# Feed-forward block 0: from the fourth weight group on, the low parts of the weights are made by GpSimd instead of VectorE

## The chip, the core and the metric

The kernel runs on one core of a Trainium2 chip. The metric is the device time of one execution in microseconds (us). TensorE (PE), VectorE (DVE), ScalarE (ACT), GpSimd (POOL) and SyncE (SP) each work through an instruction queue of their own, in order, and wait for each other through semaphores. GpSimd has two jobs here: it computes, and it issues one of the two large families of DMAs (SyncE issues the other).

## The reference, cut to what matters

A residual block of 2048 tokens and 576 channels, with a modulation by `c` and two sublayers. The first is a long convolution (S4D: a kernel `K` is generated from `log_A_real`, `A_imag`, `C` and `log_dt`, and applied by FFT); the second is a dense feed-forward layer with a hidden width of 4608 and ReLU:

```python
h = _layernorm(x) * (1 + ca) + sa
x = x + ga * _A_ref(h, ...)            # long convolution, output gated
h = _layernorm(x) * (1 + cb) + sb
x = x + gb * (maximum(h @ w1, 0) @ w2)  # 576 -> 4608 -> 576
```

Everything is float32. The kernel reaches that precision on TensorE with a rounded format, float32r: an operand is split into a high part (the value rounded to float32r) and a low part (the value minus the high part), and a product is made of three: high by high, high by low, low by high.

## The kernel before, in words

The tokens are cut into NB = 4 blocks of 512. The feed-forward layer goes block by block, and the hidden width goes in NF = 36 groups of 128, so that there are 144 groups in all, numbered `g`. A group has 14 matmuls of 128x512 into the hidden tile `hps` (`first`, line 1217 in the profile of before), a ReLU on ScalarE that gives the high part `hh` (L1222), one VectorE instruction that gives the low part `hl` (L1223), and 14 matmuls of 128x512 into five accumulators `acc0` to `acc4` (`second`, L1242), two groups later.

**Weights.** A group has a tile of `w1` (128x640) and one of `w2` (128x576). SyncE loads the raw values into `r1` (L1176) and `r2` (L1180), ScalarE copies them to the high part (`split1`, L1192, and `split2`, L1201), and VectorE subtracts the high from the raw part to get the low part (in the profile all of these have line 490, that of the helper `v`, and read `w<-r,w`). `split1(g + 2)` and `split2(g)` are called in turn `g` of the main loop, and the tiles are used in turn `g + 2`, so that each is asked for two groups ahead of its use. The low parts are made only in block 0 (`g < NF`): they are also stored to `L1d` and `L2d` (L1293, from SyncE), and blocks 1 to 3 load them from there. `r1`, `r2`, `w1` and `w2` have three buffers each, so that the load of a raw tile waits until the low part of the third group before it has been made.

**Beside the feed-forward of a block** runs the convolution of the next one. For block 0 this is `block0()`: first `kg.rest`, which makes the rest of the convolution kernel (VectorE multiplies in `rot`, L389 to L395, then small TensorE products `kps<-W1r,W2r`, L421), then the storing of the kernel `kd` to memory and its loading as `kt`, and `conv(1)`: transforms on TensorE (`ps_f`, L725), butterflies and products on VectorE (tiles `W`, `U`, `K`, `Y`, `T`, `V`, all with line 490), and the inverse transform on TensorE (`ps_i`, L955). After the second inverse come the layer norm and the transposes (`ps_t`, L1006) that make block 1's operands `xh`, `xl`, `xs`. Block 1's first matmul waits for `xs`.

**GpSimd's queue** holds in this part of the program only DMA issues: loads for `kg.rest` (`W`, `Zr`, `W2r`, L379 to L381), stores of spectra (`Ud`, `Rd`, `Kd`, L716), and loads of spectra (`Ua`, `Ka`, `R`, L712). An issue that waits for its data or its buffer holds up what stands behind it. In conv(1) `Us`, `Ks` and `Vs` of the two halves p = 0 and 1 of the channels are handled one after the other; the product of half p (`product`, `Y` and `T`) needs `Ua<-Ud_0_p` and `Ka`, which come back from memory.

**Order.** The program is written as generators, which `step` advances by small pieces; then a scheduler places all instructions of an engine in one order, by their dependencies and by its own estimate of what each instruction takes. Thus moving one instruction to another engine also changes the order in which others stand, on every engine.

Of the kernel before, what the change touches and what calls it, by code (L numbers as in the profile page):

```python
# [14 lines left out]
ALU = mybir.AluOpType  # L15
# [5 lines left out]
D = 576  # L21
# [446 lines left out]
class Body:  # L468
# [20 lines left out]
    def v(self, *args, **kw):  # L489
        return self.kept(self.nc.vector.tensor_tensor(*args, **kw))  # L490
# [675 lines left out]
    def ffn(self, gens):  # L1166

        nc, I, ff = self.nc, self.I, self.ff
        v = self.v
# [8 lines left out]
        def load_r2(g):  # L1178
            r2[g] = ff.tile([P, D], F32, tag="r2", bufs=3, name="r2")
            self.kept(nc.sync.dma_start(out=r2[g], in_=I["w2"][(g % NF) * P : (g % NF) * P + P, :]))  # L1180

        def low1(g):
            w = w1[g] = ff.tile([P, 2, 5, P], F32R, tag="w1", bufs=3, name="w1")
            if g >= NF:
                nc.sync.dma_start(
                    out=w[:, 1].rearrange("p k c -> p (k c)").bitcast(F32), in_=self.L1d[g % NF]
                )

        def split1(g):

            w, r = w1[g], r1.pop(g)
            nc.scalar.activation(w[:, 0], r, AF.Copy)  # L1192
            if g < NF:
                v(w[:, 1], r, w[:, 0], op=ALU.subtract)
                late.append((self.L1d[g], w[:, 1].rearrange("p k c -> p (k c)")))

        def split2(g):

            w = w2[g] = ff.tile([P, 1152], F32R, tag="w2", bufs=3, name="w2")
            r = r2.pop(g)  # L1200
            nc.scalar.activation(w[:, 0:D], r, AF.Copy)  # L1201
            if g < NF:
                v(w[:, D:640], r[:, 512:D], w[:, 512:D], op=ALU.subtract)
                v(w[:, 640:], r[:, :512], w[:, :512], op=ALU.subtract)
                late.append((self.L2d[g], w[:, D:]))
            else:
                nc.sync.dma_start(out=w[:, D:].bitcast(F32), in_=self.L2d[g % NF])
# [71 lines left out]
        for g in range(3):  # L1279
            low1(g)  # L1280
        split1(0)
        split2(0)
        split1(1)
        yield
        waiting = []
        for g in range(n + 2):
            if g < n:
                if g + 3 < n:
                    load_r1(g + 3)
                if g + 2 < n:  # L1290
                    load_r2(g + 2)
                for dst, src in late:
                    nc.sync.dma_start(out=dst, in_=src.bitcast(F32))  # L1293
                late.clear()
                if g:
                    split2(g)
                if g and g + 2 < n:
                    split1(g + 2)
                waiting.append((g, *first(g)))
                if g == 0:  # L1300
                    split1(2)
                if g + 3 < n:
                    low1(g + 3)
                step(g)
# [164 lines left out]
```

## Time and profile before

| | |
|---|---|
| median of 3 runs | 1395.86 us (1393.40 to 1396.19) |
| the profiled execution | 1396.13 us |
| its span, first to last instruction | 1394.4 us |
| mean granted TensorE clock | 0.937 |
| PE busy | 1233.8 us, 88% |
| DVE busy | 877.9 us, 63% |
| ACT busy | 500.6 us, 36% |
| POOL busy | 197.0 us, 14% |

The feed-forward of block 0 goes from 237 us (the first `hps` matmul) to 585 us (the first `hps` matmul of block 1) of the span. Before that lie the set-up and the convolution of block 0, behind it blocks 1 to 3.

How to read the rows shown further on. A row of groups reads: line, engine, operation, output<-inputs by the program's names (buffer numbers left out), shapes, xcount | busy us in all, mean ns of one | idle time of the engine just before them, and what ended it. A row of the timeline reads: start in us, length in us, engine, line, operation, tiles, xcount, and in brackets the idle time before it and who ended it; consecutive instructions of one kind are merged. A row of stretches reads: from:to in us, length, then busy us and (xcount) of PE, PEld (weight load), DVE, ACT and POOL, then the granted TensorE clock, the share of the DMA engines and GB/s. A row of waits reads: engine, tile and line that waited <- whom it waited for: us in all, times, the longest. Consecutive VectorE instructions overlap by some 0.08 us in the records, so that several in a row take a little less than their count by their mean.

### The profile page before, as it was taken

What the parts mean: (1) busy time and instruction counts of PE and PEld (TensorE: products, weight loads), DVE (VectorE), ACT (ScalarE), POOL (GpSimd) and SP (SyncE); (2) the same over time, 40 slices, a digit from 0 to 9 for tenths busy, and PEclk for the clock granted to TensorE, in tenths of its full rate; (3) what the DMA queues carried; (4) which work ended last, traced back from release to release, by engine and by line L of the source; (5) the groups of instructions that cost most, each with busy time, mean ns of one, the idle gap of its engine ahead of it and who ended that gap; (6) DMA issues with size and microseconds to landing.
All of it is one profiled execution on the core that took longest, in us unless ns stands there. A gap on an engine that the chain in (4) does not pass through costs nothing. (4 is left out here: it accounts for less than half of the span.)

```text
span 1394.4 us, 26020 instructions
## 1 busy us (share of the span) xinstructions
PE 1233.8 (88%) x10600; PEld 978.6 (70%) x10600; DVE 877.9 (63%) x1352; ACT 500.6 (36%) x1006; POOL 197.0 (14%) x268
## 2 busy tenths in 40 slices
PE   5124677999999988889999989999999999999998
PEld 3123455777787767567777877777887878888886
DVE  5978968999885698659834978264899332101011
ACT  6975224222223322422234314543322353323231
POOL 1877311011111101021011010000010000000000
PEclk9555688999999999899999999999999999999999
DMA  6665778688878859499778996676988656666651
GB/s 191 237 240 210 274 278 308 230 297 310 286 277 276 307 196 343 148 314 343 253 244 305 339 347 198 188 251 194 377 310 308 194 161 204 204 199 195 199 176 60
DMA packets 136040, 347.55 MB, mean 249 GB/s; under 512 B 23472, under 2 KB 23760, under 8 KB 135920
## 3 DMA queue, kind: packets, MB, share of 16 engines
q1 hardware_dynamic: 108688, 222.75, 49.3%
q0 software_dynamic: 26944, 122.55, 23.9%
q8 instruction: 83, 1.36, 0.4%
q10 hardware_dynamic: 288, 0.59, 0.1%
q14 instruction: 37, 0.30, 0.1%
HBM read 264.44 MB, written 81.40 MB: 248 GB/s over the span
## 5 line engine op out<-in xcount | busy, mean ns | idle before, releaser
L1242 PE MATMUL acc<-hh,w 128*128 128x512 f32 x1296 | 424.3, 402 | 5.7 <-DVE w L490 5.7
L1217 PE MATMUL hps<-xh,w 128*128 128x512 f32 x1152 | 393.1, 401 | 0.4 <-ACT xh L1018 0.4
L1242 PEld LDWEIGHTS acc<-hh,w 128*128 128x128 f32 x1296 | 243.4, 189 | 59.6 <-DVE w L490 7.4
L1242 PE MATMUL acc<-hl,w 128*128 128x512 f32 x720 | 279.4, 400 | 0.0
L1223 DVE SCALAR_TENSOR_TENSOR hl<-hps,hh 128x512 fp32r<-128x512 f32 x144 | 98.7, 685 | 284.2 <-ACT hh L1222 284.0
L1217 PEld LDWEIGHTS hps<-xh,w 128*128 128x128 f32 x1152 | 216.5, 189 | 47.4 <-ACT xh L1018 1.2
L1217 PE MATMUL hps<-xl,w 128*128 128x512 f32 x576 | 229.8, 399 | 0.2 <-DVE xl L1023 0.2
L1222 ACT ACTIVATE hh<-hps 128x512 fp32r<-128x512 f32 x144 | 86.0, 598 | 339.7 <-PE hps L1217 336.8
L1201 ACT ACTIVATE w<-r 128x576 fp32r<-128x576 f32 x144 | 98.7, 686 | 225.7 <-issue 176.7
L1242 PEld LDWEIGHTS acc<-hl,w 128*128 128x128 f32 x720 | 135.7, 189 | 28.5
L1217 PEld LDWEIGHTS hps<-xl,w 128*128 128x128 f32 x576 | 108.8, 189 | 24.2 <-DVE xl L1023 0.5
L246 PE MATMUL kps<-W,W 128*32 128x16 f32 x2304 | 40.0, 218 | 90.8 <-POOL W L59 58.8
L1192 ACT ACTIVATE w<-r 128x640 fp32r<-128x640 f32 x144 | 105.4, 732 | 26.2 <-DMA r<-in_w_dram 25.0
L246 PEld LDWEIGHTS kps<-W,W 128*32 128x32 f32 x2304 | 37.7, 151 | 94.1 <-POOL W L59 60.1
L1217 PE MATMUL hps<-xs,w 128*128 128x512 f32 x288 | 97.3, 418 | 6.2 <-DVE hl L1223 5.5
L421 PEld LDWEIGHTS kps<-W1r,W2r 128*32 128x32 f32 x3456 | 68.9, 146 | 35.0 <-issue 21.3
L421 PE MATMUL kps<-W1r,W2r 128*32 128x48 f32 (+2 forms) x3456 | 78.0, 238 | 11.2 <-issue 5.9
L490 DVE TENSOR_TENSOR Y<-Y,T 128x1152 f32<-128x1152 f32 x64 | 84.9, 1349 | 0.2
L1217 PEld LDWEIGHTS hps<-xs,w 128*128 128x128 f32 x288 | 53.6, 192 | 20.2 <-DVE hl L1223 7.5
L726 ACT ACTIVATE Z<-ps_f 128x288 f32<-128x288 f32 x104 | 42.1, 408 | 69.0 <-PE ps_f L725 63.0
L490 DVE TENSOR_TENSOR w<-r,w 128x512 fp32r<-128x512 f32 (+2 forms) x108 | 57.8, 570 | 8.7 <-ACT w L1201 8.7
L955 PE MATMUL ps_i<-V,gc 128*128 128x288 f32 x136 | 45.4, 469 | 15.2 <-DVE x L490 12.6
(203 smaller groups left out, 1368.5 us busy)
## 6 DMA issues: line engine op xcount, KB each, us to landing
r<-in_w_dram SPq DMA_DIRECT2D x144, 320.0 KB, 4.0
r<-in_w_dram SPq DMA_DIRECT2D x144, 288.0 KB, 3.6
w<-L1d SPq DMA_DIRECT2D x108, 320.0 KB, 3.0
w<-L2d SPq DMA_DIRECT2D x108, 288.0 KB, 3.4
W2r<-W2d POOLq DMA_DIRECT2D x18, 1536.0 KB, 9.0
W2d<-W SPq DMA_DIRECT2D x12, 1536.0 KB, 7.7
Ua<-Ud POOLq DMA_DIRECT2D x15, 1152.0 KB, 11.1
W<-W1d POOLq DMA_DIRECT2D x18, 768.0 KB, 9.0
```

The lines of the kernel that those rows point to most:

```text
L246: self.nc.tensor.matmul(ps[32 * dd : 32 * dd + 32, 12 * u + q, :], W2[:, r, :, ch], W1[:, u, :, r, ch], start=(r == 0), stop=(r == 1),)
L421: nc.tensor.matmul(ps[32 * dd : 32 * dd + 32, q, :], W2[:, r, :, ch], W1[:, :na, r, ch], start=(r == 0), stop=(r == 1),)
L490: return self.kept(self.nc.vector.tensor_tensor(*args, **kw))
L726: nc.scalar.activation(Z[:, n2, c], ps[:, :PC], AF.Copy)
L955: self.nc.tensor.matmul(ps[:, :PC], a, b, start=(i == 0), stop=(i == len(todo) - 1))
L1192: nc.scalar.activation(w[:, 0], r, AF.Copy)
L1201: nc.scalar.activation(w[:, 0:D], r, AF.Copy)
L1217: nc.tensor.matmul(ps, a, x, start=(i == 0), stop=(i == 13))
L1222: nc.scalar.activation(hh, ps, AF.Relu)
L1223: nc.vector.scalar_tensor_tensor(hl, ps, 0.0, hh, op0=ALU.max, op1=ALU.subtract)
L1242: nc.tensor.matmul(acc[i], a, x, start=(f == 0 and j in (0, 3, 6, 9, 12)), stop=(f == NF - 1 and j in (2, 5, 8, 11, 13)),)
```

## The change

Both splits no longer call VectorE's subtract themselves but a new helper `low`, which takes VectorE for the groups 0 to 2 and GpSimd for the groups 3 to 35. Operands, results, tiles, buffers and the stores behind them stay as they are. Each group has three such subtracts: 128x640 for `w1`, and 128x64 and 128x512 for `w2`. So 33 x 3 = 99 instructions change the engine.

```diff
@@ -1179,6 +1179,10 @@ def ffn
+        def low(g, out, r, hi):
+            f = v if g < 3 else nc.gpsimd.tensor_tensor
+            f(out, r, hi, op=ALU.subtract)
+
@@ -1191,7 +1195,7 @@ def split1
             nc.scalar.activation(w[:, 0], r, AF.Copy)
             if g < NF:
-                v(w[:, 1], r, w[:, 0], op=ALU.subtract)
+                low(g, w[:, 1], r, w[:, 0])
                 late.append((self.L1d[g], w[:, 1].rearrange("p k c -> p (k c)")))
@@ -1200,8 +1204,8 @@ def split2
             nc.scalar.activation(w[:, 0:D], r, AF.Copy)
             if g < NF:
-                v(w[:, D:640], r[:, 512:D], w[:, 512:D], op=ALU.subtract)
-                v(w[:, 640:], r[:, :512], w[:, :512], op=ALU.subtract)
+                low(g, w[:, D:640], r[:, 512:D], w[:, 512:D])
+                low(g, w[:, 640:], r[:, :512], w[:, :512])
                 late.append((self.L2d[g], w[:, D:]))
```

In the changed kernel all lines behind the new helper stand four lines lower: L1217 becomes L1221, L1242 becomes L1246, and so on; the subtracts on GpSimd have line L1184.

## The prediction, before the changed kernel was run

> **What bounds the kernel now.** First I read the waits of TensorE, since it is busy for 88% of the span; then the stretches of block 0; then, in the stretch where it waits, what VectorE and GpSimd do. In the view of stretches the columns are from:to, length, busy us of PE, PEld, DVE, ACT and POOL with counts, granted clock, DMA share, GB/s:
>
> ```profile
> 250.00:400.00 150.00, 144.80 (x2324) 114.65 (x2323) 136.62 (x143) 34.20 (x64) 19.73 (x30) 0.99 0.78 271
> 400.00:490.00 90.00, 88.45 (x715) 67.18 (x714) 61.59 (x110) 31.77 (x67) 13.98 (x20) 1.00 0.87 301
> 490.00:564.00 74.00, 61.03 (x259) 47.87 (x258) 67.65 (x86) 16.63 (x28) 4.50 (x6) 0.98 0.68 246
> 564.00:585.00 21.00, 20.20 (x76) 14.87 (x76) 13.04 (x39) 10.41 (x21) 0.00 (x0) 0.84 0.63 201
> 1200.00:1225.00 25.00, 25.00 (x112) 20.71 (x111) 2.58 (x4) 7.56 (x12) 0.00 (x0) 1.00 0.68 199
> ```
>
> Up to 490 us and again from 564 us TensorE is busy nearly all the time. Only from 490 to 564 is it idle for 13.0 us, and there VectorE is busy for 67.65 of 74 us. The last row, from block 3, gives the price of a matmul of 128x512 where nothing disturbs: 25 us / 112 = 0.223 us.
>
> Whom TensorE waits for between 490 and 585 us (total, times, longest):
>
> ```profile
> PE acc L1242 <- DVE w L490: 5.7, 3, 5.0
> PE hps L1217 <- DVE hl L1223: 5.1, 3, 2.0
> PE ps_i L955 <- DVE V L490: 2.6, 1, 2.6
> ```
>
> The first row is the one that the change takes away. But the longest of these waits is directly followed by the one for `V`, which is the input of the second inverse transform: TensorE gets there by 561 us and `V` is there at 564 us. From `V` the way goes through `ps_i`, norm and transposes to block 1. So what sets block 0's end is when VectorE has made `V`, plus the TensorE work that stands behind `ps_i` in its queue. The waits for `w` and `hl` before it are time that TensorE would have spent waiting for `V` instead.
>
> What lies on VectorE's way to `V`, from the groups of VectorE between 490 and 564 us:
>
> ```profile
> L490 DVE TENSOR_TENSOR T<-Ka,Ua 128x1152 f32<-128x1152 f32 x4 | 5.2, 1352 | 2.9 <-issue 2.9
> L490 DVE TENSOR_TENSOR T<-K,Ua 128x1152 f32<-128x1152 f32 x4 | 5.2, 1352 | 3.0 <-DMA Ua<-Ud 3.0
> L490 DVE TENSOR_TENSOR Y<-K,Ua 128x1152 f32<-128x1152 f32 x4 | 5.2, 1350 | 5.3 <-issue 5.3
> L490 DVE TENSOR_TENSOR w<-r,w 128x640 fp32r<-128x640 f32 x6 | 4.9, 815 | 0.0
> L1223 DVE SCALAR_TENSOR_TENSOR hl<-hps,hh 128x512 fp32r<-128x512 f32 x7 | 4.8, 681 | 0.0
> L490 DVE TENSOR_TENSOR w<-r,w 128x512 fp32r<-128x512 f32 x6 | 4.1, 682 | 0.0
> L490 DVE TENSOR_TENSOR x<-ps_i,x 128x288 f32<-128x288 f32 x4 | 1.8, 451 | 0.1
> L490 DVE TENSOR_TENSOR w<-r,w 128x64 fp32r<-128x64 f32 x7 | 1.5, 215 | 0.0
> ```
>
> The low parts are 4.9 + 4.1 + 1.5 = 10.5 us of it, and 5.3 + 3.0 + 2.9 = 11.2 us are idle, each time ahead of a product that reads `Ua`, a load that GpSimd issues. GpSimd's timeline around them:
>
> ```profile
> 475.15 0.77 POOL L716 DMA_DIRECT2D Rd<-K  x1 [4.05 <-DVE K L490]
> 478.41 0.76 POOL L716 DMA_DIRECT2D Kd<-K  x1 [2.48 <-DVE K L861]
> 479.16 0.76 POOL L712 DMA_DIRECT2D Ua<-Ud  x1
> 509.27 0.75 POOL L712 DMA_DIRECT2D R<-Rd  x1 [28.61 <-DVE T L490]
> 524.18 0.76 POOL L716 DMA_DIRECT2D Rd<-K  x1 [14.16 <-DVE K L490]
> 524.93 0.75 POOL L712 DMA_DIRECT2D Ua<-Ud  x1
> 528.68 0.76 POOL L716 DMA_DIRECT2D Kd<-K  x1 [2.99 <-DVE K L861]
> 529.43 0.75 POOL L712 DMA_DIRECT2D Ka<-Rd  x1
> DMA to landing us min/median/max: 6.8/11.1/19.9
> ```
>
> The last row is that of `Ua`'s transfers. Issued at 479.16 and 524.93, with 11.1 us they are there at 490.3 and 536.0, where VectorE's idle times end. So VectorE's way to `V` is pinned at two points to the time at which GpSimd issues.
>
> **The change, part by part.** *The new instructions.* GpSimd's subtract of these sizes isn't in the trace; the nearest rows are its other two-input instructions:
>
> ```profile
> L59 POOL TENSOR_TENSOR W<-c,E 128x384 f32<-128x384 f32 x36 | 35.8, 1017 | 8.3 <-ACT c L56 8.3
> L59 POOL TENSOR_TENSOR zs<-zs,E 128x192 f32<-128x192 f32 x12 | 7.1, 609 | 0.0
> L59 POOL TENSOR_TENSOR h<-h,m_sa 128x576 f32<-128x576 f32 x4 | 5.7, 1417 | 0.2
> ```
>
> From 192 to 576 elements: (1417 - 609) / 384 = 2.10 ns an element. So 1.55 us for 640, 1.28 for 512 and 0.34 for 64: 3.17 us a group, against 0.815 + 0.682 + 0.215 = 1.71 us on VectorE. The Trainium skill, GPSIMD Reference, section Performance versus the Vector engine, gives 4497 ns for 2048 elements, from which 1216 elements would be an estimated 2.67 us; six groups would be 16.0 us instead of 19.0, and my forecast about 1 us lower.
>
> *Do the two engines work side by side?* VectorE and GpSimd where both read two operands from SBUF, and then each kind alone:
>
> ```profile
> 158.44 4.76 DVE L490 TENSOR_TENSOR W<-ZU 128x576 f32<-128x576 f32 x4
> 157.01 4.91 POOL L59 TENSOR_TENSOR W<-T,T 128x384 f32<-128x384 f32 x4 [6.09 <-issue]
> 510.89 2.76 DVE L490 TENSOR_TENSOR W<-Y 128x576 f32<-128x576 f32 x4
> 52.23 3.03 DVE L125 SCALAR_TENSOR_TENSOR k<-th,k 128x192 f32<-128x192 f32 x11
> 53.18 3.34 POOL L59 TENSOR_TENSOR h<-h,m_ca 128x576 f32<-128x576 f32 x1 [3.86 <-DVE k L125]
> ```
>
> Four VectorE instructions of one size take 2.76 us alone and 4.76 us while two of GpSimd's run: 2.0 us more, about the two GpSimd instructions' own 2 x 1.02 us. In the last pair it is the other way round: VectorE's run isn't slowed, and GpSimd's instruction takes 3.34 us instead of 1.42. Either way they take turns. So a moved subtract isn't free: except where VectorE is idle or reads an operand from PSUM (`hl`, `x`), its 3.17 us go against VectorE's products. The Trainium skill says this too (GPSIMD Reference, Specifications: contention with instructions of VectorE that have two SBUF inputs), while Advanced Engine Details and Errata, VectorE Performance Modes, speaks only of instructions in a two-port mode; by that alone nothing here would conflict, which is the second rival. The rows decide for the wider rule.
>
> *250 to 400 us.* The rows of VectorE there:
>
> ```profile
> L391 DVE TENSOR_TENSOR W1r<-W,Zr 128x1536 f32<-128x1536 f32 x16 | 27.8, 1750 | 13.4 <-PE kps L421 13.4
> L490 DVE TENSOR_TENSOR w<-r,w 128x640 fp32r<-128x640 f32 x15 | 12.2, 815 | 0.0
> L1223 DVE SCALAR_TENSOR_TENSOR hl<-hps,hh 128x512 fp32r<-128x512 f32 x15 | 10.2, 680 | 0.0
> L490 DVE TENSOR_TENSOR w<-r,w 128x512 fp32r<-128x512 f32 x14 | 9.5, 680 | 0.0
> L490 DVE TENSOR_TENSOR w<-r,w 128x64 fp32r<-128x64 f32 x14 | 3.0, 214 | 0.0
> ```
>
> 14 groups x 3.17 = 44.4 us of GpSimd, of which `hl` can cover 10.2; 34.2 us stand against the 12.2 + 9.5 + 3.0 = 24.7 us that VectorE gets rid of plus its 13.4 us of waiting for TensorE, 38.1 in all. It fits, barely. But TensorE's order now asks for VectorE's results earlier. Here is the place in its queue of the first product `kps_5052` of the last kernel item; `hps_5038` and `hps_5224` are two groups' hidden tiles in turn. Before:
>
> ```order
> L1217 MATMUL hps_5224<-xh_0_2820,w1_4796 128x512 x2
> L1217 MATMUL hps_5224<-xl_0_2821,w1_4796 128x512
> L1217 MATMUL hps_5224<-xh_0_2820,w1_4796 128x512
> L421 MATMUL kps_5052<-W1r_11_4906,W2r_11_4886 32x16
> L1217 MATMUL hps_5224<-xh_0_2820,w1_4796 128x512
> ```
>
> and after:
>
> ```order
> L1221 MATMUL hps_5038<-xs_0_2822,w1_4693 128x512 x2
> L1221 MATMUL hps_5038<-xh_0_2820,w1_4693 128x512
> L1221 MATMUL hps_5038<-xl_0_2821,w1_4693 128x512
> L1221 MATMUL hps_5038<-xh_0_2820,w1_4693 128x512 x2
> L1221 MATMUL hps_5038<-xl_0_2821,w1_4693 128x512
> L421 MATMUL kps_5052<-W1r_11_4906,W2r_11_4886 32x16 x48
> ```
>
> It has moved ahead by 18 matmuls of `hps` and 19 of `acc`, 37 x 0.223 = 8.3 us of work. VectorE was ahead of TensorE here (its 13.4 us are waits for TensorE). Without that lead each us late is a wait of TensorE, which is busy for 144.8 of 150 us and can't make it up. Between 0 and 8.3 us I take 2, near the lower end, as the sum fits.
>
> *400 to 490 us.* VectorE is busy for 61.6 of 90 us; the lows find room. Nothing, while that room is there; the fourth rival has what it costs if the queue blocks.
>
> *490 to 564 us.* Six groups x 3.17 = 19.0 us of GpSimd. `hl` and `x` cover 4.8 + 1.8; of the 11.2 idle I count half, 5.6, since a low comes when its group comes. 6.8 us are left against 10.5 removed: VectorE gains 3.7 us. Bounds: 10.5 gained (no conflict) and 8.5 lost (no cover). Now the DMAs. GpSimd's queue at the second `Ua` (`Rd`, `Kd` are stores of the spectra `K`, `K2`), before:
>
> ```order
> L712 DMA R_5849<-Rd_0_1_110 128x4x576
> L716 DMA Rd_1_1_112<-K_1_1_5851 128x4x576
> L712 DMA Ua_5957<-Ud_0_1_102 128x4x576
> L716 DMA Kd_0_1_116<-K2_1_1_5914 128x4x576
> L712 DMA Ka_5979<-Rd_0_1_110 128x4x576
> ```
>
> and after:
>
> ```order
> L712 DMA R_5849<-Rd_0_1_110 128x4x576
> L1184 TENSOR_TENSOR w1_5931<-r1_5892,w1_5931 128x640
> L1184 TENSOR_TENSOR w2_5965<-r2_5831,w2_5965 128x64
> L1184 TENSOR_TENSOR w2_5965<-r2_5831,w2_5965 128x512
> L1184 TENSOR_TENSOR w1_5996<-r1_5959,w1_5996 128x640
> L716 DMA Rd_1_1_112<-K_1_1_5851 128x4x576
> L716 DMA Kd_0_1_116<-K2_1_1_5914 128x4x576
> L712 DMA Ua_5957<-Ud_0_1_102 128x4x576
> L712 DMA Ka_5979<-Rd_0_1_110 128x4x576
> ```
>
> `Ua` now stands behind `Kd`, which waits for `K2`. With VectorE as before it would go at 529.43, not 524.93: 4.5 us late. At the first `Ua` three lows, 3.17 us, now stand between `Rd` and `Kd`, where GpSimd waited 2.48 us: 1 us late. So: VectorE starts 1 us late at 490 and has gained some 1.7 of its 3.7 us by `K2`; `Ua` goes at 528.7, lands 3.8 us later than before, and takes back more than was gained; at the third idle 0.5 us less and the 2.9 us idle absorb the rest. `V` comes when it came: 0. By the bounds: -4 (10.5 gained, and the issues follow `K2`) to +9.
>
> *Behind `V`.* The first `ps_i` of the second inverse in TensorE's queue, before:
>
> ```order
> L1242 MATMUL acc4_0_3044<-hl_6109,w2_6081 128x512
> L1242 MATMUL acc0_0_3040<-hh_6167,w2_6139 128x512
> L1242 MATMUL acc1_0_3041<-hh_6167,w2_6139 128x512
> L1242 MATMUL acc2_0_3042<-hh_6167,w2_6139 128x512
> L1242 MATMUL acc3_0_3043<-hh_6167,w2_6139 128x512
> L1242 MATMUL acc4_0_3044<-hh_6167,w2_6139 128x512
> L955 MATMUL ps_i_6153<-V_1_1_6095,gc_1928 128x288 x2
> ```
>
> and after:
>
> ```order
> L1246 MATMUL acc4_0_3044<-hh_6108,w2_6081 128x512
> L1221 MATMUL hps_6242<-xs_0_2822,w1_6053 128x512 x2
> L1221 MATMUL hps_6242<-xh_0_2820,w1_6053 128x512
> L1221 MATMUL hps_6242<-xl_0_2821,w1_6053 128x512
> L1221 MATMUL hps_6242<-xh_0_2820,w1_6053 128x512 x2
> L1221 MATMUL hps_6242<-xl_0_2821,w1_6053 128x512
> L955 MATMUL ps_i_6153<-V_1_1_6095,gc_1928 128x288 x2
> ```
>
> Seven matmuls of `hps_6242`, five of `w2_6081` (its `hl`) and five of `w2_6139` stood ahead of `ps_i` and now stand behind it: 17 x 0.223 = 3.8 us more to do once `V` is there.
>
> **The sum:** 2 + 0 + 3.8 = +5.8 us on the profiled execution's 1396.1 us (span 1394.4 and 1.7 around it), which lies 0.3 us above the median of the runs: 1402 us.
>
> **The rivals.** *Second: no conflict to speak of, but the transfers hold.* `V` 4 us earlier, 3.8 us more behind it, no wait before 400: 1396 us. For it: in the pair at 53 us VectorE wasn't slowed. Against it: the pair at 158 us.
>
> *Third, faster: VectorE's 10.5 us come through whole.* `V` 10.5 us earlier and 3.8 us of work behind it: -6.7, 1389 us. It needs the transfers of `Ua` in well under 11.1 us (6.8 is the shortest seen), and decides from where `V` is ready before 560 us. The 13 us of TensorE's idle time speak for it; the two pinned issues against it.
>
> *Fourth: the lows wait in GpSimd's queue.* An issue that waits for VectorE holds up the lows behind it: 28.61 us before `R` in the row above. 36 groups in 348 us are 9.7 us each, so the lead is 19.3 us; one such wait costs TensorE 9.3 us, with the forecast's 5.8 us 1411 us. The order puts lows ahead of and behind such issues, which speaks against it.
>
> **How the numbers follow.** Forecast 0.5, second 0.22, third 0.15, fourth 0.13. 0.2% is 2.8 us, about what a measurement can tell here. Slower: the forecast and the fourth, less a little: 0.6; same: the second: 0.23; faster: the third and a tail: 0.17. The forecast's own range is 1396 to 1410; the range given reaches to the third's centre, 1390, and past the fourth's, 1416.
>
> **What would show it.** Right: no wait of `acc` for `w`, a longer one of `ps_i` for `V`; `V` ready as far behind the first `hps` as now (327 us) or later; products of VectorE that take longer than 1.35 us while GpSimd subtracts. Wrong: `V` much earlier, or waits of TensorE for GpSimd's `w`.

## The result, and the profile after

The changed kernel is slower: 1417.75 us median (1415.23 to 1421.07, 4 runs) against 1394.63 us before (1390.06 to 1396.19, 4 runs), a ratio of 1.0169 with a 95% interval of 1.0144 to 1.0195. The predicted sign was right and the size was not: 1402 us was predicted, +5.8 us on before, with a range to 1416.

The profiled execution after has a span of 1416.5 us, 22.1 more than before. Nearly all of it is lost in block 0: from the first `hps` of block 0 to the first of block 1 it takes 369.1 us (235.2 to 604.3), before 347.7 (237.2 to 584.9), so 21.4 more. I follow the loss by the start of a group's first `hps`, counted from that of group 0. Group 20 came at 192.2 us before and at 205.5 after: 13.3 us are lost by then, and 8.1 behind it. From the first `hps` of block 0 to that of block 1, before and after:

```profile
237.20:584.90 347.70, 326.97 (x3416) 254.33 (x3416) 290.72 (x390) 101.59 (x192) 38.20 (x55) 0.98 0.78 273
235.20:604.30 369.10, 326.16 (x3399) 253.63 (x3399) 294.46 (x291) 100.20 (x189) 193.20 (x157) 0.94 0.73 255
```

TensorE is busy for as long as before (with 18 matmuls fewer, at a lower granted clock), and its idle time goes from 20.7 to 42.9 us: the loss is waiting.

The stretches of after, with the columns of the prediction's table:

```profile
250.00:400.00 150.00, 133.34 (x2142) 105.35 (x2143) 144.84 (x97) 31.25 (x58) 86.81 (x69) 0.97 0.80 278
400.00:490.00 90.00, 88.18 (x845) 67.97 (x843) 58.36 (x81) 29.63 (x63) 46.77 (x45) 1.00 0.77 264
490.00:564.00 74.00, 67.64 (x272) 53.23 (x271) 44.34 (x48) 19.45 (x35) 48.70 (x35) 0.93 0.70 244
564.00:605.00 41.00, 23.44 (x93) 17.48 (x93) 33.11 (x53) 11.77 (x23) 4.24 (x4) 0.75 0.51 181
```

In the first row VectorE, which got rid of 24.7 us of subtracts here, is busier than before (144.84 us against 136.62, with 97 instructions against 143), and TensorE has lost 11.5 us (133.34 against 144.80). In the last row TensorE is idle for 17.6 of 41 us; before it was idle for 0.8 of the 21 us to block 1's first matmul.

The reason stands in VectorE's groups, 250 to 430 us. Before:

```profile
L391 DVE TENSOR_TENSOR W1r<-W,Zr 128x1536 f32<-128x1536 f32 x17 | 29.6, 1750 | 13.4 <-PE kps L421 13.4
L395 DVE TENSOR_TENSOR W1r<-W1r,T 128x768 f32<-128x768 f32 x24 | 22.7, 947 | 0.0
L393 DVE TENSOR_TENSOR W1r<-W1r,T 128x768 f32<-128x768 f32 x23 | 21.8, 947 | 0.0
...
L391 DVE TENSOR_TENSOR W1r<-W1r,Zr 128x1536 f32<-128x1536 f32 x6 | 10.5, 1748 | 0.0
```

and after:

```profile
L395 DVE TENSOR_TENSOR W1r<-W1r,T 128x768 f32<-128x768 f32 x24 | 36.0, 1500 | 0.0
...
L393 DVE TENSOR_TENSOR W1r<-W1r,T 128x768 f32<-128x768 f32 x24 | 31.4, 1309 | 0.2
L391 DVE TENSOR_TENSOR W1r<-W,Zr 128x1536 f32<-128x1536 f32 x16 | 28.2, 1775 | 3.0 <-PE kps L421 2.9
L391 DVE TENSOR_TENSOR W1r<-W1r,Zr 128x1536 f32<-128x1536 f32 x6 | 15.5, 2590 | 0.0
...
L1227 DVE SCALAR_TENSOR_TENSOR hl<-hps,hh 128x512 fp32r<-128x512 f32 x18 | 12.3, 681 | 1.7 <-ACT hh L1226 1.7
```

The same instructions take up to 1.6 times as long, though not all of them: `W1r<-W,Zr` takes 1775 ns on average, hardly more than its 1750. `hl`, which reads one operand from PSUM (the memory that TensorE writes; the other tiles here lie in SBUF), takes 681 ns, before 679. Summed over the multiplies, subtracts and adds of `rot` (L389 to L395) that start between 250 and 400 us, it is 31.6 us more than they take alone. And the 13.4 us for which VectorE waited for `kps` are 2.9: it was ahead of TensorE, and now TensorE waits for it. How two instructions meet is seen in the timeline (start, length):

```profile
264.77 1.99 POOL L1184 TENSOR_TENSOR w<-r,w 128x512 fp32r<-128x512 f32 x1
...
265.55 2.03 DVE L395 TENSOR_TENSOR W1r<-W1r,T 128x768 f32<-128x768 f32 x1
...
268.01 1.59 POOL L1184 TENSOR_TENSOR w<-r,w 128x640 fp32r<-128x640 f32 x1 [1.25 <-ACT w L1196]
268.10 3.12 DVE L389 TENSOR_TENSOR T<-W,Zr 128x1536 f32<-128x1536 f32 x1
...
272.61 0.95 DVE L395 TENSOR_TENSOR W1r<-W1r,T 128x768 f32<-128x768 f32 x1
```

At 268 us GpSimd's subtract starts 0.09 us ahead, and VectorE's multiply takes 1.4 us more than its own 1.75, about the 1.5 us that the subtract still has to run. At 272.61 GpSimd computes nothing beside it, and `L395` takes its 0.95 us.

TensorE's waits between 250 and 400 us, after:

```profile
PE kps L421 <- issue: 9.4, 6, 2.8
PE hps L1221 <- DVE hl L1227: 4.7, 2, 2.5
PE kps L421 <- DVE W1r L395: 1.5, 3, 1.0
PE kps L421 <- ACT w L1196: 1.1, 1, 1.1
```

The same before:

```profile
PE kps L421 <- issue: 4.7, 4, 2.0
PE hps L1217 <- DVE hl L1223: 0.5, 1, 0.5
```

The waits add up to 16.7 us after and 5.2 before, and the difference is the 11.5 us that TensorE lost. "issue" names no releaser. By the program's dependencies a `kps` can start only when its part of VectorE's `W1r` is complete: the three waits put down to `L395` end 0.05 us behind the end of such an instruction, and the two longest "issue" waits (2.7 and 2.8 us) 0.10 us behind the end of an `L393`, which also writes `W1r`. What ended the other four, 3.9 us, the trace doesn't show.

GpSimd between 486 and 550 us:

```profile
485.83 0.79 POOL L716 DMA_DIRECT2D Rd<-K  x1 [2.39 <-DVE K L490]
487.57 4.17 POOL L1184 TENSOR_TENSOR w<-r,w 128x64 fp32r<-128x64 f32 x3 [0.96 <-ACT w L1205]
...
492.46 0.75 POOL L712 DMA_DIRECT2D Ua<-Ud  x1
...
494.94 3.09 POOL L1184 TENSOR_TENSOR w<-r,w 128x64 fp32r<-128x64 f32 x3 [0.99 <-ACT w L1205]
500.87 1.55 POOL L1184 TENSOR_TENSOR w<-r,w 128x640 fp32r<-128x640 f32 x1 [2.84 <-ACT w L1196]
...
532.35 13.80 POOL L1184 TENSOR_TENSOR w<-r,w 128x640 fp32r<-128x640 f32 x4 [4.97 <-ACT w L1196]
546.09 0.77 POOL L716 DMA_DIRECT2D Rd<-K  x1
...
547.61 0.75 POOL L712 DMA_DIRECT2D Ua<-Ud  x1
```

Where VectorE waits, a whole group takes 3.09 us, as priced. Beside VectorE's products four subtracts (640, 64, 512, 640 elements) stretch from 1.55 + 0.34 + 1.28 + 1.55 = 4.7 us to 13.80, and the second `Ua` stands behind them. The first of the four alone takes 8.53 us, from 532.35 to 540.88. VectorE at that time:

```profile
531.08 2.89 DVE L490 TENSOR_TENSOR V<-W 128x576 f32<-128x576 f32 x6
533.89 2.75 DVE L490 TENSOR_TENSOR W<-Z 128x576 f32<-128x576 f32 x4
536.56 2.89 DVE L490 TENSOR_TENSOR K<-W 128x576 f32<-128x576 f32 x6
539.37 0.45 DVE L490 TENSOR_TENSOR x<-ps_i,x 128x288 f32<-128x288 f32 x1
539.74 2.36 DVE L859 SCALAR_TENSOR_TENSOR K<-R,sgn,K 128x1152 f32<-128x1152 f32 x1
```

VectorE's run of instructions with two SBUF operands isn't slowed at all (`V` takes 2.89 us in before too, four `W` 2.76), and the subtract ends 1.5 us, its own length, behind the start of `x`, which reads an operand from PSUM; the instruction behind `x` is the one that is slowed (2.36 us, before 1.40). What follows on VectorE and TensorE once `Ua` is there:

```profile
563.48 2.76 DVE L490 TENSOR_TENSOR T<-K,Ua 128x1152 f32<-128x1152 f32 x2 [12.41 <-DMA Ua<-Ud]
...
582.54 0.69 DVE L1227 SCALAR_TENSOR_TENSOR hl<-hps,hh 128x512 fp32r<-128x512 f32 x1
...
583.28 1.22 PE L1221 MATMUL hps<-xs,w 128*128 128x512 f32 x2 [17.48 <-DVE hl L1227]
...
585.82 2.90 DVE L490 TENSOR_TENSOR V<-W 128x576 f32<-128x576 f32 x6
```

`hl` stands in VectorE's queue behind the products that wait for `Ua`; the next matmul in TensorE's queue waits for this `hl`, and TensorE idles for 17.48 us.

### The profile page after: what moved, and what is told of

Read it like the earlier page. It is cut to its first block, busy times and chain, and to the rows that moved or that the text cites. A ratio compares the mean times of both kernels' runs of the same rounds, so it can differ in the third digit from the quotient of the medians.

```text
span 1416.5 us, 26045 instructions
## 1 busy us (share of the span) xinstructions
PE 1235.1 (87%) x10600; PEld 979.5 (69%) x10600; DVE 882.4 (62%) x1253; ACT 501.0 (35%) x1006; POOL 348.9 (25%) x367
## 4 chain that ended last, share of the span: by engine, by line
PE 58%; DVE 25%; DMA 7%; issue 5%; POOL 2%; ACT 2%; DVEq 0%; SPq 0%; POOLq 0%; ACTq 0%
PE hps L1221 22%; PE acc L1246 22%; DVE Y L490 5%; DVE T L490 4%; DMA Ua<-Ud 4%; PE kps L421 4%; PE ps_f L725 3%; DVE W1r L391 2%; DVE T L389 2%; PE ps_i L955 2%; DVE W L490 2%; DVE W1r L395 2%; DMA Ud<-U 1%; PE kps L246 1%; DVE hl L1227 1%
## 5 line engine op out<-in xcount | busy, mean ns | idle before, releaser
L1246 PE MATMUL acc<-hh,w 128*128 128x512 f32 x1296 | 432.6, 402 | 0.0
L1221 PE MATMUL hps<-xh,w 128*128 128x512 f32 x1152 | 397.7, 405 | 0.0
L1246 PE MATMUL acc<-hl,w 128*128 128x512 f32 x720 | 286.9, 400 | 0.0
L1246 PEld LDWEIGHTS acc<-hh,w 128*128 128x128 f32 x1296 | 242.9, 189 | 52.5
L1221 PEld LDWEIGHTS hps<-xh,w 128*128 128x128 f32 x1152 | 218.6, 191 | 48.5 <-ACT xh L1018 1.2
L1221 PE MATMUL hps<-xl,w 128*128 128x512 f32 x576 | 229.7, 399 | 0.5 <-DVE xl L1023 0.5
L1184 POOL TENSOR_TENSOR w<-r,w 128x64 fp32r<-128x64 f32 (+2 forms) x99 | 153.7, 1570 | 124.3 <-ACT w L1205 73.2
L1246 PEld LDWEIGHTS acc<-hl,w 128*128 128x128 f32 x720 | 136.0, 189 | 28.4
L1221 PEld LDWEIGHTS hps<-xl,w 128*128 128x128 f32 x576 | 110.1, 191 | 25.6 <-DVE xl L1023 2.2
L1221 PE MATMUL hps<-xs,w 128*128 128x512 f32 x288 | 98.4, 420 | 29.3 <-DVE hl L1227 28.5
L421 PEld LDWEIGHTS kps<-W1r,W2r 128*32 128x32 f32 x3456 | 68.2, 146 | 42.8 <-issue 23.5
L490 DVE TENSOR_TENSOR Y<-Y,T 128x1152 f32<-128x1152 f32 x64 | 88.7, 1409 | 0.2
L1221 PEld LDWEIGHTS hps<-xs,w 128*128 128x128 f32 x288 | 53.8, 192 | 42.5 <-DVE hl L1227 30.8
L490 DVE TENSOR_TENSOR W<-Z 128x576 f32<-128x576 f32 x52 | 37.1, 759 | 43.7 <-ACT Z L726 43.7
## 6 DMA issues: line engine op xcount, KB each, us to landing
Ua<-Ud POOLq DMA_DIRECT2D x15, 1152.0 KB, 11.2
```

The lines of the kernel that those rows point to most:

```text
L421: nc.tensor.matmul(ps[32 * dd : 32 * dd + 32, q, :], W2[:, r, :, ch], W1[:, :na, r, ch], start=(r == 0), stop=(r == 1),)
L1184: f(out, r, hi, op=ALU.subtract)
L1221: nc.tensor.matmul(ps, a, x, start=(i == 0), stop=(i == 13))
L1246: nc.tensor.matmul(acc[i], a, x, start=(f == 0 and j in (0, 3, 6, 9, 12)), stop=(f == NF - 1 and j in (2, 5, 8, 11, 13)),)
```

## The experiments

Three theories. **1**: GpSimd's subtracts and VectorE's instructions with two SBUF operands hold each other up, and that makes VectorE the bound. **2**: the other order that the scheduler makes, above all on TensorE, costs by itself. **3**: the subtracts delay the DMA issues behind them in GpSimd's queue. In the table, group 20's start (behind group 0's) and the length of block 0 are from one profiled execution each; the ratio is that of the timed runs to the kernel before, with its 95% interval. Block 0's length ends at block 1's first matmul, and not as many matmuls stand ahead of it in every kernel: 2216 in the program of before, 2198 in the changed kernel's, 2188 in e9's (the records of a trace are more). At 0.223 us each, a kernel with the new order has up to 4 to 6 us less in this column for work that it does later; the ratios don't have this.

| kernel | group 20, us | block 0, us | ratio |
|---|---|---|---|
| before | 192.2 | 347.7 | 1 |
| changed | 205.5 | 369.1 | 1.0169 (1.0144 to 1.0195) |
| e1_early: GpSimd for groups 3 to 19 | 205.0 | 358.9 | 1.0053 (1.0008 to 1.0097) |
| e2_late: GpSimd from group 20 on | 195.2 | 357.0 | 1.0073 (1.0031 to 1.0116) |
| e3_dup: GpSimd in addition to VectorE | 211.7 | 385.4 | 1.0249 (1.0204 to 1.0294) |
| e4_act: ScalarE copies, no subtract | 191.8 | 340.1 | 0.9970 (0.9925 to 1.0015) |
| e5_w1only: GpSimd for the 640s alone | 196.4 | 352.2 | 1.0043 (1.0016 to 1.0069) |
| e6_copy: GpSimd copies, no subtract | 200.3 | 356.9 | 1.0076 (1.0052 to 1.0100) |
| e7_spafter: changed, Ka and Ua from SyncE | 205.2 | 359.6 | 1.0127 (1.0076 to 1.0177) |
| e8_spbefore: before, Ka and Ua from SyncE | 190.6 | 339.2 | 0.9963 (0.9939 to 0.9986) |
| e9_spall: changed, all loads from SyncE | 206.8 | 365.6 | 1.0147 (1.0125 to 1.0169) |
| e10_spallbefore: before, all loads from SyncE | 195.9 | 344.1 | 0.9964 (0.9943 to 0.9984) |
| e11_spcopy: e6 with all loads from SyncE | 188.3 | 339.9 | 0.9963 (0.9945 to 0.9982) |
| e12_spcopy2: e11, each copy made twice | 190.2 | 343.6 | 0.9979 (0.9956 to 1.0002) |

**Early groups alone, and late groups alone.**

```diff
-            f = v if g < 3 else nc.gpsimd.tensor_tensor
+            f = nc.gpsimd.tensor_tensor if 3 <= g < 20 else v    # e1_early
+            f = nc.gpsimd.tensor_tensor if g >= 20 else v        # e2_late
```

> GpSimd makes the low parts for groups 3 to 19 alone, VectorE those of 0 to 2 and 20 to 35. Theory 1 (GpSimd's subtracts and VectorE's operations with two SBUF inputs hold each other up, and VectorE becomes the bound from 250 to 430 us): group 20 starts 11 to 15 us later behind the first group than before, nothing more is lost behind it, total 1394 + 11 to 15 = 1405 to 1410. Theory 2 (the loss is the other order of the TensorE queue: here the first transform's matmuls stand as in the changed kernel): the same 1405 to 1410 here, so these two are told apart by the two kernels below. Theory 3 (the low parts delay the DMA issues that stand behind them in GpSimd's queue, before the second inverse transform's input): 1394 to 1397.

> GpSimd makes the low parts from group 20 on alone. Theory 1: the stretch 250 to 400 is as before (group 20 at 192 +- 2 us behind the first); what is lost comes from 440 us on, by VectorE's slower products and by the issues behind the low parts: 1400 to 1406; with the kernel for groups 3 to 19 its loss adds up to the changed kernel's 23. Theory 2: the TensorE queue stands nearly as before, so 1394 to 1397. Theory 3: the whole loss, 1414 to 1418.

The early groups alone cost 12.8 us by group 20 (205.0 against 192.2) and 11.2 us in block 0; the late ones 3.0 and 9.3 us. Together that is 20.5 of the changed kernel's 21.4 us: the loss is made in both parts. The timed runs agree less exactly, 0.53% and 0.73% against 1.69%. Theory 1 expected group 20 of the late kernel at 192 +- 2 us, and it came at 195.2; and of the early kernel 11 to 15 us, of which its ratio shows 7 (1 to 14 by the interval). Theory 3 alone (nothing early, all of it late) falls. Theories 1 and 2 are not told apart by these two.

**The subtracts twice, and none.** In the first kernel VectorE keeps its work and GpSimd does it again, into a scratch tile that nobody reads. In the second GpSimd computes nothing here: ScalarE writes the low parts, with another value.

```diff
# e3_dup
-            f = v if g < 3 else nc.gpsimd.tensor_tensor
-            f(out, r, hi, op=ALU.subtract)
+            v(out, r, hi, op=ALU.subtract)
+            if g > 2:
...
+                    t = ff.tile([P, 320], F32R, tag="dup", bufs=1, name="dup")
+                    nc.gpsimd.tensor_tensor(t[:, : e - k], x[:, k:e], y[:, k:e], op=ALU.subtract)
# e4_act
-            f = v if g < 3 else nc.gpsimd.tensor_tensor
-            f(out, r, hi, op=ALU.subtract)
+            if g < 3:
+                v(out, r, hi, op=ALU.subtract)
+            else:
+                nc.scalar.activation(out, r, AF.Copy)
```

> VectorE makes all low parts as before; GpSimd makes those of groups 3 to 35 a second time, into a scratch tile that nobody reads (in pieces of 320 elements). The order of the TensorE queue is that of the kernel before. Theory 1: VectorE has its old work and the hold-ups on top, so the loss by group 20 is larger than the changed kernel's 13 (20 to 40 us), total 1425 to 1450. Theory 2: 1393 to 1398. Theory 3: only the issues are late, 1400 to 1406.

> From group 3 on ScalarE fills the low part with a plain copy of the loaded weights, in place of the subtract: VectorE is relieved of the same work, GpSimd computes nothing, the TensorE queue stands as in the changed kernel; the values of the low parts are other ones. Theory 1: no hold-up, so group 20 comes at 188 to 194 us behind the first, total 1385 to 1396. Theory 2: 1408 to 1418, as in the changed kernel. Theory 3: 1390 to 1396, as no low part stands ahead of the issues; theories 1 and 3 are told apart by the other three kernels.

I compare orders by the fewest matmuls that have to be moved to turn one into the other, among those that both do from block 0's first `hps` to block 1's. From before's 2216 to the first kernel it is 10, to the second 363 (to the changed kernel 360), and from the changed kernel to the second 13. So the first has the old order with GpSimd's subtracts, the second the new order without them. The first loses 19.5 us by group 20 and 37.7 in block 0, the second nothing by group 20, and it is 7.6 us shorter in block 0, of which 4.0 are the 18 matmuls that it does later. Theory 2 falls: the new order costs nothing while VectorE is fast. VectorE's rows in the first, 250 to 430 us, show that its own subtracts (814 ns before) suffer too:

```profile
L395 DVE TENSOR_TENSOR W1r<-W1r,T 128x768 f32<-128x768 f32 x22 | 25.9, 1179 | 0.0
...
L490 DVE TENSOR_TENSOR w<-r,w 128x640 fp32r<-128x640 f32 x15 | 19.6, 1309 | 0.0
```

In the second kernel VectorE is busy for 123.73 us and TensorE for 144.26:

```profile
250.00:400.00 150.00, 144.26 (x2284) 114.36 (x2283) 123.73 (x105) 55.07 (x109) 19.52 (x29) 0.99 0.84 289
```

This is also about the most that relieving VectorE can bring here (ScalarE has 99 copies more in this kernel, so it is no exact bound). With 13 us less of VectorE's work in this stretch than before, and no cost on GpSimd, the time is 0.9970 of before with an interval that holds 1: TensorE is the bound, as the first table of the prediction says.

**Half the dose.** Only the raw tile of `w1` has three dimensions in the program, so that the condition picks its subtract.

```diff
-            f = v if g < 3 else nc.gpsimd.tensor_tensor
+            f = nc.gpsimd.tensor_tensor if g > 2 and len(r.shape) == 3 else v
```

> Half a dose: from group 3 on GpSimd subtracts for the first weights alone (640 of the 1216 elements a group), VectorE for the second. Theory 1 (the hold-ups between GpSimd's subtracts and VectorE's operations with two SBUF inputs): about half of the changed kernel's loss of 21 us in block 0, 8 to 13 us, total 1403 to 1409. A theory by which any GpSimd subtract in the queue moves the order and the order alone costs: the whole loss or none; the two kernels with and without GpSimd's work have already spoken against it.

Block 0 is 4.5 us longer, not 8 to 13: the cost grows faster than the dose, and the ratio (1.0043, at most 1.0069) is also under half of 1.0169's excess. That fits a bound that VectorE reaches only once its slack is gone, but this run alone does not show it.

**One SBUF operand in place of two.** Where ScalarE made a copy in the kernel above, GpSimd makes it here; the order on TensorE is that of the changed kernel but for 11 matmuls, counted as above.

```diff
-            f = v if g < 3 else nc.gpsimd.tensor_tensor
-            f(out, r, hi, op=ALU.subtract)
+            if g < 3:
+                v(out, r, hi, op=ALU.subtract)
+            else:
+                nc.gpsimd.tensor_copy(out, r)
```

> From group 3 on GpSimd fills the low part with a plain copy of the loaded weights: one SBUF input in place of two, at the same place in its queue, with the TensorE queue of the changed kernel; the values of the low parts are other ones. Theory 1a (only two SBUF inputs on both sides collide): VectorE's operations keep their alone durations (953 ns for 768 elements), group 20 at 188 to 195 us, block 0 at 340 to 350 us. Theory 1b (any GpSimd operation that reads SBUF collides): VectorE's operations overlapped by the copies are longer, group 20 at 198 to 206. Theory 3 (the late second inverse transform comes from DMA issues behind GpSimd's work, whatever it computes): group 20 as before but block 0 at 352 to 360 us.

No theory got this one whole. VectorE is only a little slower (`L395` 1096 ns on average against 947 before and 1500 in the changed kernel), yet 8.1 us are lost by group 20. The stretch and VectorE's longest wait in it:

```profile
250.00:400.00 150.00, 139.35 (x2258) 110.29 (x2257) 126.94 (x99) 33.28 (x61) 72.89 (x72) 0.97 0.84 290
```

```profile
DVE T L389 <- DMA Zr<-Zd: 18.8, 4, 7.7
```

VectorE isn't full, it waits for the load of `Zr`, which GpSimd issues between its copies. So theory 3 holds for this kernel, and in a part of the program that I had not thought of. It calls for the next runs.

**The loads from another queue.** First `Ka` and `Ua` of the product alone, in the changed kernel and in that of before; then also the loads for `kg.rest`, in both and in the copying kernel.

```diff
+        q = self.nc.sync if name in ("Ka1", "Ua1") else self.nc.gpsimd
-        self.nc.gpsimd.dma_start(out=t.rearrange("p a b c -> p a (b c)"), in_=strips(src, 4))
+        q.dma_start(out=t.rearrange("p a b c -> p a (b c)"), in_=strips(src, 4))
...
-                Ka = Ks[p] if t == 0 else self.load(self.Kd[s - t][p], "Ka")
+                Ka = Ks[p] if t == 0 else self.load(self.Kd[s - t][p], "Ka1" if s == 1 else "Ka")
...
-                d = nc.gpsimd.dma_start
+                d = (nc.sync if items[0][1] == (1, 2, 3) else nc.gpsimd).dma_start
```

`Ua` gets its name in the same way. The last edit, for `kg.rest`, is only in the kernels with all loads moved.

> The changed kernel with the loads of the spectra for the first convolution's product (Ka, Ua) issued from SyncE's queue and not behind the low parts in GpSimd's. Theory 3: the second inverse transform's input comes 8 to 12 us earlier than in the changed kernel, block 0 at 357 to 362 us, total 1405 to 1410. Theory 1 (slower VectorE alone): block 0 at 366 to 371, total 1413 to 1418.

> The control of the run ahead: the kernel before with the same two loads on SyncE's queue. Theory 1 and theory 3 alike: 1392 to 1398, block 0 at 345 to 350 us; if SyncE's queue itself holds the loads up (it issues the weights and the stores that wait for low parts), later, and the run ahead is to be read against this one.

> The changed kernel with all loads of block 0 that stand among the low parts in GpSimd's queue issued from SyncE's instead: W, Zr and W2r of the kernel transform (L379 to L381) and Ka, Ua of the first convolution. If the loss is VectorE's held-up operations alone (theory 1): as the changed kernel with only the late loads moved, block 0 at 356 to 361 us, VectorE busy 143 to 150 of 150 us at 250 to 400. If the loads behind the low parts are part of the loss at 250 to 400 too (theory 3): group 20 at 195 to 201 us behind the first and block 0 at 345 to 354.

> The kernel in which GpSimd copies (one SBUF input) in place of subtracting, with the same loads moved to SyncE's queue; the values of the low parts are other ones. Its loss without the move was 8 us by group 20 and 9 in block 0, with VectorE at 127 of 150 us busy and 18.8 us of waits for Zr. Theory 3: these waits go, group 20 at 189 to 194 us, block 0 at 335 to 345. If the loss is not the queue's: group 20 again at 198 to 202, block 0 at 353 to 358.

> The control: the kernel before with the same loads on SyncE's queue. Both theories: as the kernel before with only Ka and Ua moved, block 0 at 337 to 343 us, total 1384 to 1391; if SyncE's queue then holds up the weights' loads (a load that waits for its buffer stands ahead of them), later than that, 345 to 355.

Read without its control, the first run would have spoken for theory 3: 9.5 us less in block 0 (359.6), as it expected. But before gains 8.5 us by the same edit (339.2), against my expectation that nothing would move. The changed kernel stays 20.4 us behind its control, and 21.5 with all loads moved (365.6 against 344.1). So the place of these loads costs both kernels something, and explains about 1 us of the difference between them; by the ratios it explains none (1.0127 to 0.9963 and 1.0147 to 0.9964 are 1.64% and 1.83%, without the move 1.69%). In the copying kernel it explains the whole loss: 356.9 becomes 339.9, and group 20 comes at 188.3.

The changed kernel with all loads moved met neither theory: 365.6 us where 356 to 361 or 345 to 354 was expected, and VectorE busy for 131.86 of 150 us, not for 143 to 150; it waits 18.0 us for `hh` there. That VectorE is full, as theory 1 has it, holds for the changed kernel (144.84), for e1_early (146.09), e3_dup (150.00) and e7_spafter (146.35), but the loss stays where it isn't. What all five have in common are VectorE's stretched instructions.

Both controls are faster than the kernel before: 0.9963 and 0.9964, intervals below 1. The version to take is the kernel before with `Ka` and `Ua` of the first convolution issued from SyncE's queue; moving more loads does not show any further gain, and its block 0 (344.1 us) is above the 337 to 343 that was expected.

**The same length of work with one operand.** A subtract of 640 elements takes 1.55 us alone, a copy 0.72. So the copies are made twice each, in the copying kernel with the loads moved:

```diff
+                nc.gpsimd.tensor_copy(out, r)
                 nc.gpsimd.tensor_copy(out, r)
```

> The kernel with one-input copies and the loads on SyncE's queue, every copy made twice: alone 2 x (0.722 + 0.620 + 0.238) = 3.16 us of GpSimd a group, as much as the subtracts' 3.17; the values of the low parts are other ones. The subtracting kernel with the same loads moved had block 0 at 365.6 us, the one with single copies 339.9. If what costs those 26 us is that the subtract reads two SBUF inputs: block 0 at 338 to 346 us, VectorE's overlapped 768-element operations at 0.95 to 1.05 us. If it is the length of GpSimd's work (late low parts, longer sharing): 356 to 367.

343.6 us, in the range for two operands; the subtracting kernel with the same loads moved takes 365.6, and the orders of the two on TensorE differ by 63 of 2188 matmuls. VectorE's operations of 768 elements are at 1165 ns, above the 0.95 to 1.05 us that went with that range. The stretch in this kernel, GpSimd's copies of 640 elements, second and first of each pair (723 ns is the median of those that overlap no VectorE instruction), and VectorE's add:

```profile
250.00:400.00 150.00, 141.15 (x2097) 113.28 (x2099) 133.62 (x107) 33.84 (x62) 105.78 (x86) 0.98 0.73 263
```

```profile
L1188 POOL CAST w<-r 128x640 fp32r<-128x640 f32 x32 | 52.0, 1625 | 1.5
...
L1187 POOL CAST w<-r 128x640 fp32r<-128x640 f32 x32 | 32.1, 1004 | 21.9 <-PE hps L1225 13.5 <-DMA r<-in_w_dram 7.7 <-issue 0.8
```

```profile
L395 DVE TENSOR_TENSOR W1r<-W1r,T 128x768 f32<-128x768 f32 x24 | 28.0, 1165 | 0.0
```

and the stretch and the add for the subtracting kernel with all loads moved:

```profile
250.00:400.00 150.00, 134.31 (x1926) 107.26 (x1927) 131.86 (x93) 30.93 (x56) 77.12 (x39) 0.92 0.70 252
```

```profile
L395 DVE TENSOR_TENSOR W1r<-W1r,T 128x768 f32<-128x768 f32 x22 | 36.1, 1642 | 0.0
```

With copies GpSimd is busy for 105.78 us beside VectorE's 133.62, and TensorE keeps 141.15; with subtracts GpSimd does 77.12 us, VectorE 131.86, and TensorE 134.31. So it isn't the length of GpSimd's work that costs the 22 us. The copies do collide (VectorE's add takes 1165 ns, not 947), but at a smaller price than the subtracts (1642). `L395` is the row that suffers most; over all of `rot` between 250 and 430 us VectorE takes 32.3 us more than alone beside the subtracts, 15.8 beside the doubled copies and 7.5 beside single ones (e11). So the price grows with GpSimd's time, but per us of it a copy costs half of a subtract, and 15.8 us cost little in block 0 (343.6 against 339.9 with single copies) where 32.3 cost 22 more. The granted clock is lower beside the subtracts too (0.92 against 0.98 in this stretch), and no run separates that from the waits. That the second SBUF operand itself makes the difference is what the pair suggests; subtract and copy also differ as operations, and no run varied the operands with the operation kept.

## Why the prediction was wrong in size

*The new instructions: right.* Predicted 3.17 us a group alone; the row at 494.94 shows 3.09, and 1.55 for 640 elements at 500.87.

*They collide: right. That they take turns: only in part.* `hl`, with an operand in PSUM, is not slowed, and five of the six rows of `rot` are. The size on VectorE's side holds: 34.2 us of conflict were set against it between 250 and 400 us (31.6 measured), less 24.7 removed, which makes +9.5 busy; it measured 144.84 - 136.62 = +8.2. On GpSimd's side nothing was set, as if each conflict cost one engine alone; its subtracts there took 68.4 us in place of the 42.8 that they take alone. The Trainium skill, GPSIMD Engine Reference, section Specifications, names this contention, and the traces agree (1500 ns against 947 for `L395`). Nor do the two-port modes, by which the second rival stood, cover all conflicts: these rows have one.

*250 to 400 us: the step that failed.* "It fits, barely", with +2 taken from 0 to 8.3; by group 20 it is +13.3. The 9.5 us were set against the 13.4 us for which VectorE waited, as if sums over 150 us could be netted. But the waits were the lead by which `W1r` was ready before TensorE came to `kps`. With the lead gone, a `kps` behind a slowed instruction of `rot` is a wait of TensorE, and as that was busy for 144.8 of 150 us it makes up none. The earlier place of `kps` was priced as the cost itself, at up to 8.3, a bound that was passed; by `e4_act` that order alone costs nothing while VectorE is fast, and the slow VectorE decides.

*400 to 490 us: right (0).* `Rd<-K` was issued 237.9 us behind the first `hps` before (475.15 - 237.2) and 250.6 after (485.83 - 235.2): +12.7, no more than group 20's +13.3.

*490 to 564 us: right in the places, and the second step that failed in size.* 0 was predicted, -4 to +9, and it was +12.0. The last `V` ends 353.5 us behind the first `hps` (588.7 - 235.2), before 328.8 (566.0 - 237.2): +24.7, of which 12.7 were lost earlier and 12.0 here. The first `Ua` goes 6.6 us behind `Rd`, before 4.0: +2.6 in place of +1. The second follows the first by 55.2 us, before 45.8: +9.4 in place of +2.8 (3.8 behind the 1.0 of the first), behind four subtracts that took 13.80 us in place of 4.7. I had priced the queue with subtracts that run alone, although the conflict was my own argument, and one of them was held for 7 us. The transfer then took 15.9 us in place of 11.1, and VectorE's way from there to `V` was shorter by as much. The controls show that this chain can't be read as the cost of the queue alone: without it the difference between the kernels stays.

*Behind `V`: wrong sign.* +3.8 was predicted; from the last `V` to block 1 it is 15.6 us (588.7 to 604.3), before 18.9. Before and after:

```profile
566.00:585.00 19.00, 18.22 (x73) 13.70 (x72) 11.04 (x35) 10.41 (x21) 0.00 (x0) 0.88 0.70 223
588.70:604.40 15.70, 15.70 (x72) 12.23 (x71) 8.42 (x29) 10.59 (x21) 1.57 (x2) 1.00 0.45 133
```

TensorE does about as many matmuls in both, not 17 more: the prediction counted what moved behind `ps_i`, but not the 18 matmuls of `acc` that moved on, behind block 1's first `hps`. In the program 51 matmuls of `hps` and `acc` stand between the two before and 50 after. What is left is the higher granted clock after. In both traces the clock is at about half behind TensorE's long waits: 0.50 from 564 to 570 us before, most of which lies behind `V`, and 0.52 from 583.0 to 588.7 after, which lies ahead of the last `V`, since TensorE was at work again 5 us ahead of it, after its 17.48 us wait for `hl`. The prediction did not have that wait: it saw what stands behind `Ua` in GpSimd's queue, not what stands behind it in VectorE's. So that this term came out below 0 is the clock in the main, which the prediction did not look at, and not a gain of the change.

*The sum.* 2 + 0 + 3.8 = 5.8 us was predicted; 12.7 + 12.0 - 3.3 = 21.4 us was measured in block 0.

*Signs named ahead.* No wait of `acc` for `w`, `V` later than 327 us behind the first `hps`, products slowed by subtracts: all there. The longer wait of `ps_i` for `V` is not; TensorE waits for `hl` instead.

*Rivals.* The second and third fall. The fourth (the lows wait in GpSimd's queue) is not there in its form, as no matmul waits for GpSimd's `w`.

## What to carry to other kernels

In these traces, moving an elementwise instruction with two SBUF operands from VectorE to GpSimd relieved VectorE only where its own instructions read an operand elsewhere or where it waited; beside products of two SBUF operands, price it as added VectorE work, and price what stands behind it in GpSimd's queue with the stretched duration. Don't net waits against work over a long stretch: if the engine that waits is the one that runs ahead of the bound, its waits are the lead that hides its delays. And give an experiment that moves a transfer its control on the kernel before: here the control had gained as much, and was the better kernel.

## What the runs showed of the hardware that was not expected

- GpSimd can be held up far beyond a turn: four subtracts worth 4.7 us took 13.80 us beside VectorE's products (532.35 in after). The first waited through 14 VectorE instructions that follow each other without a gap, and got its 1.5 us at the first one that reads PSUM.
- GpSimd's copies with one SBUF operand collide as well, but VectorE loses less: `L395` takes 947 ns without them, 1165 beside doubled copies, 1500 to 1642 beside subtracts. The Trainium skill, SBUF — State Buffer, section Who interferes with whom, describes the shared ports as a lock that a VectorE instruction with two SBUF inputs and any GpSimd instruction that reads SBUF take from each other; the traces agree that both kinds collide (GpSimd's 640-element copies go from 723 ns to 1004 and 1625 on average), and show a price that differs by kind.
- Five loads of 1152 KB issued from SyncE's queue in place of GpSimd's (the order on TensorE then differs by 74 matmuls) made block 0 of the kernel before 8.5 us shorter, of which 2.5 are 11 matmuls done later (ratio 0.9963, 0.9939 to 0.9986). Whether the earlier issue, the queue or the order does it, no run separates.
- The granted clock of TensorE was 0.50 while it did nothing (570 to 583 us in after) and 0.52 in the 5.7 us of work behind that.
